# A fused convolution and feed-forward kernel on Trainium2: blocks 2 and 3 convolved in bf16 quarter tiles, and two chunks of F in one PSUM tile

## The chip, the cores and the metric

The kernel runs on one core of one Trainium2 chip. The metric is device microseconds of one execution; lower is better. A core has TensorE (PE: matmuls; its weight loads are shown apart as PEld), VectorE (DVE), ScalarE (ACT), GpSimd (POOL) and SyncE (SP), each with an instruction queue that it works off in order, and 16 DMA engines. DMAs are issued from the queues of SP, ACT and POOL. SBUF holds 128 partitions of working data; PSUM takes the results of matmuls, in banks of 512 fp32 a partition.

## The reference, cut to what matters

```python
w = softmax(weight, axis=-1)                     # 8 heads x 7 taps
x_unf = x_pad[:, arange(S)[:, None] + arange(7)[None, :], :]   # 6 zeros ahead of each sequence
y = einsum('hk,bskhg->bshg', w, x_unf)           # causal convolution, one set of taps a head
h = y.reshape(32768, 192) @ w_in                 # 192 -> 2048
g = h * (1.0 / (1.0 + exp(-beta * h)))           # beta: one number for each of the 2048
out = g @ w_out                                  # 2048 -> 192
```
There are 8 sequences of 4096 tokens with 192 features; all is fp32 outside, the kernel's matmuls of the two large products are bf16.

## The kernel before, in words

The 32768 tokens are two *streams* of 16384, worked side by side: s = 0 on one half of the partitions, s = 1 on the other. The 192 features are split in three groups of 64 (`NK = 3`, `Q = 64`), so that a convolved tile `xc` has 2 x 64 partitions and three groups by tokens in the free dimensions. F = 2048 is 16 chunks of 128 (`NF`).

The kernel goes through *steps*, ranges of tokens of each stream: step 0 and 1 have 128 tokens, step 2 256, steps 3 to 5 256 each, steps 6 and 7 384, then 512 each. In each step three things are computed:

- the convolution. From step 3 on VectorE does it in seven tap operations (`conv_ops`, L276) on `xt`, the transposed x; the work of later steps stands in a list that `vector_work` (L484) deals out by a budget of nanoseconds for each chunk. For the first four blocks of 128 tokens (steps 0 to 2) TensorE does it: x is transposed on TensorE (`transpose_0`), taken into `xr` in fp32r (`take_0`), and multiplied by seven diagonal matrices `diag` of the taps, one pair of matmuls a tap, one for each stream (`conv_0`, L225). `evac_0` takes the result from PSUM, scaled by `rsum`, to `xcp`.
- mm1: `xc` times w_in, into a PSUM tile `ph` of [128, 2, 512] (two of them rotate), and Silu on ScalarE with the scale `beta`, into `g`. Steps 0 to 2 use `mm1_pair` (L318): chunks u and u + 8 together, chunk u on partition half 0 and u + 8 on half 1, both streams in one moving operand. The others use `mm1` (L333): one chunk a PSUM tile, stream 0 on half 0 and stream 1 on half 1; steps of 256 tokens fill half of the tile.
- mm2: `g` times w_out, in the steps up to 5 by `mm2` (L366): a chunk's 128 rows in two halves, two matmuls of 64x192 for two blocks of 128 tokens, summed over 16 chunks and two phases in two PSUM banks `po`; then `store` copies them out (`o_sp`) and SP writes them. Later steps use `mm2_quarters`, which is untouched. `mm2_plan` (L355) deals four chunks of mm2 of the step before to each chunk of mm1; for steps 0 and 1 the table `first_mm2` (L547) says which chunks of mm2 go behind which unit (i, u).

`mm1_pair` reads only that half of F that lies on its partition half: w_in_s[half 0] holds F 0 to 1023, half 1 the rest. For `mm1` both halves need all of F: `copy_w_in` (L115, issued at L252) copies each half to the other on chip by four DMAs from POOL's queue.

Every instruction is kept in program order on its engine (`pin`), so the order around the change is written by hand. POOL's queue holds, in this order: w_in in six transfers (F 0-255 of each half, 256-639, then the two x loads of blocks 2 and 3 into `xb0`, then 640-1023), w_out_f in four, `xb1` (tokens 512 to 767) in two, `xf` in two, the four copies of w_in_s. `first_tile(i, u)` (L499) says what else is done in steps 0 and 1, behind mm1 of chunk pair u: block 1's convolution at (0,1) and (0,2), its eviction and the transposes of blocks 2 and 3 at (0,3), block 2's convolution at (0,5) and (0,6), block 3's at (1,0) and (1,1), the transposes of xb1 at (1,6), casts and DMA transposes for tile 1 at (1,7). The 16 multiplications of w_out by 1/beta (`scale_w_out`) stand between them on VectorE.

Of the kernel before, what the change touches and what calls it, by code (L numbers as in the profile page):

```python
# [19 lines left out]
def kernel(  # L20
# [25 lines left out]
    def pin(ins):  # L46

        return tc.keep_in_program_order(ins)
# [16 lines left out]

    steps = [(0, 128), (128, 128), (256, 256)]
    NP = len(steps)
# [82 lines left out]
    for f0, f1 in ((0, 256), (256, 640), (640, HF)):  # L150
        for s in range(NS):
            load_w_in(s, HF * s + f0, HF * s + f1)
        if f0 == 256:
            for b in range(2, NB):
                load_x0(b, nc.gpsimd)
# [9 lines left out]
    xr = consts.tile([128, NK, PAD + TILE], FP32R, name="xr")  # L165
# [27 lines left out]
    etap = consts.tile([128, K], FP32, name="etap")  # L193
# [11 lines left out]
    place = [(0, 0), (1, 0), (2, 0), (2, 128)]  # L205
    for i in range(NP):
        xc_of[i] = xc_pool.tile([128, NS, NK, steps[i][1]], BF16, name=f"xcp{i}", bufs=1)
# [10 lines left out]
    def take_0(t, b, act=False):  # L218
        dst = xr[:, :, PAD + 128 * b:PAD + 128 * b + 128]
        if act:  # L220
            pin(nc.scalar.activation(dst, t, AF.Copy))
        else:
            pin(nc.vector.tensor_copy(dst, t))
# [9 lines left out]
    def evac_0(cv, b, s, eng, k0=0, k1=NK):  # L233
        i, c = place[b]
        src = cv[s][:, 128 * k0:128 * k1].rearrange("p (k t) -> p k t", t=128)
        dst = xc_of[i][:, s, k0:k1, c:c + 128]
        if eng is nc.scalar:
            pin(nc.scalar.activation(dst, src, AF.Copy, scale=rsum))
        else:
            pin(eng.tensor_scalar_mul(dst, src, rsum))  # L240
# [11 lines left out]
    for f in range(0, HF, 512):  # L252
        for s in range(NS):
            copy_w_in(s, HF * s + f, HF * s + f + 512)
# [15 lines left out]
    pin(nc.vector.tensor_scalar_mul(tapn, etap, rsum))  # L270

# [61 lines left out]
    def mm1(i, fc):  # L333


        n = steps[i][1]
        ph = psum_h.tile([128, NS, TILE], FP32, name="ph")
        parts = [(0, 128)] if i <= NQ else [(0, 64), (64, 128)]
        for kk in range(NK):
            for m0, m1 in parts:  # L340
                for s in range(NS):
                    pin(nc.tensor.matmul(ph[m0:m1, s, 0:n],  # L342
                                         w_in_s[half_of(s), kk, 128 * fc + m0:128 * fc + m1],
                                         xc_of[i][half_of(s), kk, 0:n],
                                         start=(kk == 0), stop=(kk == NK - 1)))
        pin(nc.scalar.activation(g_at(i, fc)[:, :, 0:n], ph[:, :, 0:n], AF.Silu,  # L346
                                 scale=beta[:, fc:fc + 1]))
# [34 lines left out]
    def store(i, pr, po):  # L382
# [5 lines left out]
        if sa == sb:  # L388
# [110 lines left out]
    def first_tile(i, u):  # L499
# [4 lines left out]
        elif (i, u) == (0, 3):  # L504
            t23 = [transpose_0(pa[b], xb0, b) for b in range(2)]
            for b in range(2):
                take_0(t23[b], 2 + b)
            for s in range(NS):
                evac_0(pb, 1, s, nc.vector)
        elif (i, u) == (0, 5):  # L510
            conv_0(pa, 2, 0, 4)
            for c in range(4):
                scale_w_out(c)
        elif (i, u) == (0, 6):
            conv_0(pa, 2, 4, K)
            for s in range(NS):
                evac_0(pa, 2, s, nc.vector)
            for c in range(4, 8):
                scale_w_out(c)
        elif (i, u) == (1, 0):  # L520
            conv_0(pb, 3, 0, 4)
        elif (i, u) == (1, 1):
            conv_0(pb, 3, 4, K)
            for s in range(NS):
                evac_0(pb, 3, s, nc.vector)
            for c in range(8, NF):
                scale_w_out(c)
        elif (i, u) == (1, 6):
            new_xt(1)
            ts_ = [transpose_0(pb[b], xb1, b) for b in range(2)]  # L530
            for b in range(2):
                pin(nc.vector.tensor_copy(xt_of[1][:, :, LEAD + 128 * b:LEAD + 128 * b + 128], ts_[b]))
            pin(nc.vector.tensor_copy(xt_of[0][:, :, TILE + LEAD - PAD:],
                                      xr[:, :, TILE:].bitcast(FP32)))
# [13 lines left out]
    for key, us, cuts in (((0, 0), [(1, u) for u in range(2, 8)], (0, 3, 6, 9, 12, 13, 16)),  # L548
                          ((1, 0), [(2, 1), (2, 2)], (0, 8, 16)),
                          ((0, 1), [(2, 3), (2, 4)], (0, 8, 16)),  # L550
                          ((1, 1), [(2, 5), (2, 6), (2, 7)], (0, 5, 10, 16))):
        for (i, u), c0, c1 in zip(us, cuts, cuts[1:]):
            first_mm2[(i, u) + key] = range(c0, c1)

    for i in range(n_steps):
        plan = mm2_plan(i - 1) if NP <= i <= NQ else [[] for _ in range(NF)]
        new_g(i, 0)
        if i < NP:
            new_g(i, 1)
        if i < NP:  # L560
            for u in range(NF // 2):
                mm1_pair(i, u)
                first_tile(i, u)
                for ph in (0, 1):
                    for j in range(i):
                        for fc in first_mm2.get((i, u, j, ph), ()):
                            mm2(j, prs_0, ph, fc)
                if i == 2:
                    vector_work(i, 1300, flush=u == NF // 2 - 1)
            continue  # L570
        for u in range(NF):
            if u == NF // 2:
                new_g(i, 1)
            mm1(i, u)
            for t in plan[u]:
                mm2(i - 1, *t)
                if t[1] == 1 and t[2] == NF - 1:
                    budget -= 2 * (D + 60) / 0.96
            if i > NQ:
                mm2_quarters(NM)  # L580
            vector_work(i, 1307 * steps[i][1] // TILE, flush=u == NF - 1)
# [30 lines left out]
```

## Time and profile before

| | |
|---|---|
| five runs | 686.74, 687.43, 687.5, 687.4, 686.19 us; median 687.4 |
| the profiled execution | 686.74 us; span 685.0 us, 1.74 us outside the span |
| granted TensorE clock | 1.000 |
| TensorE busy | 679.1 us, 99% of the span |
| ScalarE, VectorE busy | 585.4 us (85%), 551.4 us (81%) |
| POOL busy | 14.6 us |

The page's numbers are of one execution. Busy time of TensorE is time in which any matmul is in flight, with modelled ends, so the gaps between starts say more than the share. "Idle before" of an instruction is the time its engine did nothing just before it, with the releaser that ended it. The timeline view merges neighbours of one line, so a row's length can reach over rows of another line. The view of DMA issues gives the time from issue to landing. The first 32 us hold steps 0 to 2; step 3 begins at 30.68 us, step 4 at 41.7, step 5 at 52.3, step 6 at 62.84 and step 7 at 76.27.

### The profile page before, as it was taken

The numbers are of one execution on the slowest core, as the hardware profiler recorded it, in microseconds if no ns is written. First come the engines' busy times: TensorE is split into PE (matmuls) and PEld (weight loads), VectorE is DVE, ScalarE is ACT, GpSimd is POOL, SyncE is SP. The second block draws the span as 40 slices with busy tenths as digits, with TensorE's granted clock in tenths as the row PEclk, the third lists the DMA queues.
The fourth block names the chain that finished last, engine by engine and source line by source line (L and its number), as shares of the span: only waits on it lengthen the run. The fifth ranks groups of instructions, "written<-read, shape, count | busy, mean of one in ns | idle before, by whom it ended". The sixth has DMA issues, their size and how long they took to land.

```text
span 685.0 us, 27204 instructions
## 1 busy us (share of the span) xinstructions
PE 679.1 (99%) x12528; PEld 460.0 (67%) x12528; DVE 551.4 (81%) x886; ACT 585.4 (85%) x585; POOL 14.6 (2%) x26
## 2 busy tenths in 40 slices
PE   8999999999999999999999999999999999999998
PEld 6799887666666666666666666666666666666667
DVE  5999999999988889878889888889888889875112
ACT  7999999888888888888888888888888888888881
POOL 8000000000000000000000000000000000000000
PEclk9999999999999999999999999999999999999999
DMA  9753444344423344423444323344323443220223
GB/s 203 185 131 92 121 110 118 85 117 117 117 61 82 103 109 117 117 53 85 106 112 117 96 63 97 100 118 117 87 58 105 105 117 72 67 51 4 49 48 94
DMA packets 150418, 66.85 MB, mean 98 GB/s; under 512 B 113648, under 2 KB 149696, under 8 KB 150304
## 3 DMA queue, kind: packets, MB, share of 16 engines
q1 hardware_dynamic: 146992, 61.08, 35.1%
q0 software_dynamic: 3168, 3.93, 2.8%
q8 instruction: 98, 1.61, 1.1%
q14 instruction: 16, 0.13, 0.1%
q10 hardware_dynamic: 144, 0.10, 0.1%
HBM read 28.32 MB, written 25.17 MB: 78 GB/s over the span
## 4 chain that ended last, share of the span: by engine, by line
PE 97%; DMA 1%; POOL 1%; ACT 1%; issue 0%; DVE 0%; POOLq 0%
PE ph L342 47%; PE po L420 43%; PE po L374 4%; PE po L458 2%; PE ph L325 1%; DMA w_in_s<-in_moe_w_in_dram 1%; ACT g L329 1%; POOL w_in_s L113 0%; PE po L229 0%; ACT gp L329 0%; POOL xb L131 0%; PE po L215 0%; POOL sel L146 0%; DVE o_sp L380 0%; POOL ident L148 0%
## 5 line engine op out<-in xcount | busy, mean ns | idle before, releaser
L346 ACT ACTIVATE g<-ph,beta 128x1024 bf16<-128x1024 f32 (+2 forms) x528 | 558.6, 1063 | 80.0 <-PE ph L342 62.0
L342 PE MATMUL ph<-xc,w_in_s 64*64 64x512 bf16 (+3 forms) x5952 | 617.5, 368 | 0.3 <-ACT g L329 0.3
L420 PE MATMUL po<-g,w_out_s 64*64 64x512 bf16 (+1 forms) x5568 | 580.9, 372 | 0.0
L342 PEld LDWEIGHTS <-w_in_s 64*64 64x64 bf16 (+1 forms) x5952 | 274.9, 104 | 126.0 <-issue 0.5
L420 PEld LDWEIGHTS <-w_out_s 64*64 64x64 bf16 x5568 | 290.1, 118 | 83.8
L303 DVE SCALAR_TENSOR_TENSOR acc<-xt,tapn,acc 128x512 f32<-128x512 bf16 (+2 forms) x450 | 311.4, 768 | 0.9
L437 DVE STREAM_TRANSPOSE o_sb<-po 128x512 f32<-128x512 f32 (+1 forms) x87 | 76.5, 880 | 112.1 <-PE po L420 112.0
L303 DVE SCALAR_TENSOR_TENSOR xc<-xt,tapn,acc 128x512 bf16<-128x512 bf16 (+2 forms) x90 | 64.2, 770 | 0.2
L87 DVE CAST xb<-xf 128x768 bf16<-128x768 f32 (+1 forms) x62 | 48.6, 824 | 0.2 <-DMA xf<-in_x_dram 0.2
L301 DVE TENSOR_SCALAR acc<-xt,tapn 128x512 f32<-128x512 bf16 (+2 forms) x90 | 41.1, 486 | 1.1
L374 PE MATMUL po<-w_out_s,g 64*128 64x192 bf16 x512 | 32.6, 243 | 0.0
L374 PEld LDWEIGHTS <-g 64*128 64x128 bf16 x512 | 24.8, 94 | 1.6
L325 PE MATMUL ph<-xcp,w_in_s 64*128 64x256 bf16 (+1 forms) x144 | 14.9, 306 | 0.8 <-DMA w_in_s<-in_moe_w_in_dram 0.6
L380 DVE COPY o_sp<-po 128x192 f32<-128x192 f32 x28 | 9.0, 353 | 8.0 <-PE po L458 7.3
L329 ACT ACTIVATE gp<-ph,beta 128x256 bf16<-128x256 f32 x32 | 12.8, 477 | 2.0 <-PE ph L325 1.8
L458 PEld LDWEIGHTS <-g 128*128 128x128 bf16 x128 | 10.5, 98 | 0.4 <-issue 0.4
L458 PE MATMUL po<-w_out_s,g 128*128 128x192 bf16 x128 | 10.7, 246 | 0.0
L329 ACT ACTIVATE g<-ph,beta 128x512 bf16<-128x512 f32 x16 | 9.6, 693 | 0.1
L325 PEld LDWEIGHTS <-w_in_s 64*128 64x128 bf16 x144 | 6.7, 94 | 4.4 <-issue 1.6
L374 PE MATMUL po<-w_out_s,gp 64*128 64x192 bf16 x128 | 7.5, 243 | 0.0
L374 PEld LDWEIGHTS <-gp 64*128 64x128 bf16 x128 | 5.9, 94 | 1.6
L229 PE MATMUL po<-xr,diag 64*128 64x384 f32 x49 | 7.0, 360 | 0.0
(52 smaller groups left out, 56.6 us busy)
## 6 DMA issues: line engine op xcount, KB each, us to landing
xf<-in_x_dram SPq DMA_DIRECT2D x60, 384.0 KB, 4.2
out_dram<-o_sb SPq DMA_DIRECT2D x108, 192.0 KB, 4.6
xt<-xb SPq DMA_TRANSPOSE x122, 3.1
out_dram<-o_sp SPq DMA_DIRECT2D x10, 192.0 KB, 3.7
w_out_f<-in_moe_w_out_dram POOLq DMA_DIRECT2D x4, 384.0 KB, 6.8
out_dram<-o_sb SPq DMA_DIRECT2D x8, 144.0 KB, 4.7
w_in_s<-w_in_s POOLq DMA_DIRECT2D x4, 192.0 KB, 7.8
out_dram<-o_sp SPq DMA_DIRECT2D x8, 96.0 KB, 1.8
```

The costliest lines, as they stand in the source:

```text
L87: pin((eng or nc.vector).tensor_copy(xbf_of[j][:, b0:b1, :, s, :].rearrange("p b k q -> p k b q"), xf_of[j][:, b0:b1, s, :].rearrange("p b ...
L301: pin(nc.vector.tensor_scalar_mul(a, src, w))
L303: pin(nc.vector.scalar_tensor_tensor(out=xc_of[i][:, k0:k1, o:o + m] if k == K - 1 else a, in0=src, scalar=w, in1=a, op0=ALU.mult, op1=ALU ...
L325: pin(nc.tensor.matmul(ph[:, h, 0:NS * n], w_in_s[half_of(h), kk, ts(fcs[h], 128)], xc_of[i][half_of(h), :, kk, :], start=(kk == 0), stop= ...
L329: pin(nc.scalar.activation(g_at(i, fcs[h])[:, :, 0:n], ph[:, h, 0:NS * n].rearrange("p (s t) -> p s t", s=NS), AF.Silu, scale=beta[:, fcs[ ...
L342: pin(nc.tensor.matmul(ph[m0:m1, s, 0:n], w_in_s[half_of(s), kk, 128 * fc + m0:128 * fc + m1], xc_of[i][half_of(s), kk, 0:n], start=(kk == ...
L346: pin(nc.scalar.activation(g_at(i, fc)[:, :, 0:n], ph[:, :, 0:n], AF.Silu, scale=beta[:, fc:fc + 1]))
L374: pin(nc.tensor.matmul(po[q][:, 0:D], g_at(i, fc)[r, s, ts(b, 128)], w_out_s[r, fc, :], start=(phase == 0 and fc == 0), stop=(phase == 1 a ...
L380: pin(nc.vector.tensor_copy(dst, po[:, 0:D]))
L420: pin(nc.tensor.matmul(po_of[i, m][half_of(s), 0:n], w_out_s[half_of(r), fc, m:D:NM], g_at(i, fc)[half_of(r), s, 0:n], start=(first and fc ...
L437: pin(nc.vector.transpose(osb_of[i][:, 0:n // L, :, m], po_of[i, m][:, 0:n].rearrange("p (b l) -> p b l", l=L)))
L458: pin(nc.tensor.matmul(po[:, 0:D], g_at(i, fc)[:, s, ts(b, 128)], w_out_s[:, fc, :], start=(fc == 0), stop=(fc == NF - 1)))
```

## The change

Blocks 0 and 1 are done as before. Blocks 2 and 3 are taken into a new bf16 tile `xrb`; their taps are split in two bf16 parts each (`tap2`: the tap, and what its rounding leaves), 14 diagonals `diag_b` in bf16, made by one VectorE instruction. `conv_23` multiplies them in quarter tiles (64 rows by 64 columns): block 2 goes to partition half 0 and block 3 to half 1, both streams in separate banks. The result `xcq` has the block as partition half, and both streams in its free dimension, so step 2 now goes through `mm1`, like the later steps, with the copies of w_in_s, and no longer through `mm1_pair`.

`mm1` takes a list of chunks: in steps of 256 tokens two chunks share one PSUM tile, and their mm2 follow behind both. The list of what is done where is written anew: the x loads of blocks 2 and 3 come behind all of w_in in POOL's queue; the copies of w_in_s are issued half by half; the transposes of blocks 2 and 3 move to (0,6) and (0,7), their convolution to (1,0) to (1,4), three diagonals each and two at last; the transposes of xb1 move from (1,6) to (1,5), with eight of the w_out multiplications behind them; mm2 of steps 0 and 1 gets another table.

```diff
     steps = [(0, 128), (128, 128), (256, 256)]
-    NP = len(steps)
+    ND, NP = 2, len(steps)
...
     for f0, f1 in ((0, 256), (256, 640), (640, HF)):
         for s in range(NS):
             load_w_in(s, HF * s + f0, HF * s + f1)
-        if f0 == 256:
-            for b in range(2, NB):
-                load_x0(b, nc.gpsimd)
+    for b in range(2, NB):
+        load_x0(b, nc.gpsimd)
...
-    xr = consts.tile([128, NK, PAD + TILE], FP32R, name="xr")
+    xr = consts.tile([128, NK, PAD + 256], FP32R, name="xr")
...
-    etap = consts.tile([128, K], FP32, name="etap")
+    tap2 = consts.tile([128, 2, K], FP32, name="tap2")
+    etap = tap2[:, 0, :]
...
+    for i in range(ND):
+        xc_of[i] = xc_pool.tile([128, NS, NK, 128], BF16, name=f"xcp{i}", bufs=1)
+    xc_of[ND] = xc_pool.tile([128, NK, NS, 128], BF16, name="xcq", bufs=1)
...
+        xd, c = (xr, PAD + 128 * b) if b < 2 else (xrb, PAD + 128 * (b - 2))
+        dst = xd[:, :, c:c + 128]
...
+    def conv_23(cv, k0, k1):
+        for k in range(k0, k1):
+            for c in range(2):
+                for s in range(NS):
+                    t = 128 * c + k % K
+                    pin(nc.tensor.matmul(
+                        cv[s][half_of(c), 0:NK * 128], diag_b[half_of(s), k, :],
+                        xrb[half_of(s), :, t:t + 128], start=(k == 0), stop=(k == 2 * K - 1)))
...
-    for f in range(0, HF, 512):
-        for s in range(NS):
+    for s in range(NS):
+        for f in range(0, HF, 512):
             copy_w_in(s, HF * s + f, HF * s + f + 512)
...
+    tap_b = consts.tile([128, K], BF16, name="tap_b")
+    pin(nc.vector.tensor_copy(tap_b, etap))
+    pin(nc.vector.tensor_tensor(out=tap2[:, 1, :], in0=etap, in1=tap_b, op=ALU.subtract))
+    diag_b = consts.tile([128, 2 * K, Q], BF16, name="diag_b")
+    pin(nc.vector.tensor_tensor(
+        out=diag_b, in0=ident2[:, None, 0, :].to_broadcast([128, 2 * K, Q]),
+        in1=tap2.rearrange("p a k -> p (a k)")[:, :, None].to_broadcast([128, 2 * K, Q]), op=ALU.mult))
+    xrb = consts.tile([128, NK, PAD + 256], BF16, name="xrb")
+    pin(nc.vector.tensor_copy(xrb[:, :, 0:PAD], xr[:, :, 256:].bitcast(FP32)))
...
-    def mm1(i, fc):
+    def mm1(i, fcs):
         n = steps[i][1]
         ph = psum_h.tile([128, NS, TILE], FP32, name="ph")
         parts = [(0, 128)] if i <= NQ else [(0, 64), (64, 128)]
+        for e, fc in enumerate(fcs):
+            for kk in range(NK):
+                for m0, m1 in parts:
+                    for s in range(NS):
+                        rhs = xc_of[i][half_of(s), kk, :, :] if i == ND else xc_of[i][half_of(s), kk, 0:n]
+                        pin(nc.tensor.matmul(ph[m0:m1, s, n * e:n * e + n],
+                                             w_in_s[half_of(s), kk, 128 * fc + m0:128 * fc + m1], rhs,
+                                             start=(kk == 0), stop=(kk == NK - 1)))
+        for e, fc in enumerate(fcs):
+            pin(nc.scalar.activation(g_at(i, fc)[:, :, 0:n], ph[:, :, n * e:n * e + n], AF.Silu,
+                                     scale=beta[:, fc:fc + 1]))
...
         elif (i, u) == (0, 3):
-            t23 = [transpose_0(pa[b], xb0, b) for b in range(2)]
-            for b in range(2):
-                take_0(t23[b], 2 + b)
             for s in range(NS):
                 evac_0(pb, 1, s, nc.vector)
-        elif (i, u) == (0, 5):
-            conv_0(pa, 2, 0, 4)
-            for c in range(4):
-                scale_w_out(c)
...
+        elif (i, u) in ((0, 6), (0, 7)):
+            b = u - 6
+            take_0(transpose_0(pa[b], xb0, b), 2 + b)
+        elif i == 1 and u < 5:
+            conv_23(pb, 3 * u, min(3 * u + 3, 2 * K))
+            if u == 0:
+                for c in range(8):
+                    scale_w_out(c)
+            elif u == 4:
+                for s in range(NS):
+                    evac_0(pb, 2, s, nc.vector)
+        elif (i, u) == (1, 5):
             new_xt(1)
             ts_ = [transpose_0(pb[b], xb1, b) for b in range(2)]
             for b in range(2):
                 pin(nc.vector.tensor_copy(xt_of[1][:, :, LEAD + 128 * b:LEAD + 128 * b + 128], ts_[b]))
             pin(nc.vector.tensor_copy(xt_of[0][:, :, TILE + LEAD - PAD:],
-                                      xr[:, :, TILE:].bitcast(FP32)))
+                                      xrb[:, :, 256:]))
+            for c in range(8, NF):
+                scale_w_out(c)
...
-    for key, us, cuts in (((0, 0), [(1, u) for u in range(2, 8)], (0, 3, 6, 9, 12, 13, 16)),
-                          ((1, 0), [(2, 1), (2, 2)], (0, 8, 16)),
-                          ((0, 1), [(2, 3), (2, 4)], (0, 8, 16)),
-                          ((1, 1), [(2, 5), (2, 6), (2, 7)], (0, 5, 10, 16))):
+    for key, us, cuts in (((0, 0), [(1, 6), (1, 7), (2, 0)], (0, 5, 10, 16)),
+                          ((1, 0), [(2, u) for u in range(2, 6)], range(0, 17, 4)),
+                          ((0, 1), [(2, u) for u in range(6, 10)], range(0, 17, 4)),
+                          ((1, 1), [(2, u) for u in range(10, 16)], (0, 2, 5, 8, 10, 13, 16))):
...
-        for u in range(NF):
+        du = 2 if steps[i][1] == 256 else 1
+        for u in range(0, NF, du):
+            us = range(u, u + du)
             if u == NF // 2:
                 new_g(i, 1)
-            mm1(i, u)
-            for t in plan[u]:
-                mm2(i - 1, *t)
+            mm1(i, us)
+            for v in us:
+                mm2_first(v)
+                for t in plan[v]:
+                    mm2(i - 1, *t)
...
-            vector_work(i, 1307 * steps[i][1] // TILE, flush=u == NF - 1)
+            vector_work(i, 1307 * du * steps[i][1] // TILE, flush=u + du == NF)
```

## The prediction

> **What bounds the kernel now.** I read the busy shares first, then the chain that ended last, then each engine's order of time in the first 32 us, since the change reaches no further than step 6.
>
> ```profile
> PE 679.1 (99%) x12528; PEld 460.0 (67%) x12528; DVE 551.4 (81%) x886; ACT 585.4 (85%) x585; POOL 14.6 (2%) x26
> ```
> ```profile
> PE 97%; DMA 1%; POOL 1%; ACT 1%; issue 0%; DVE 0%; POOLq 0%
> ```
> TensorE sets the end. From step 3 on it issues one chunk every 0.66 us without a gap, and later stages also show no wait, so a change in the head moves the end by as much as it moves step 3's stream. The head is different. TensorE, in order of time (start, length, what, idle before it and its releaser):
>
> ```profile
> 12.33 0.39 PE L325 MATMUL ph<-xcp,w_in_s 64*128 64x256 bf16 x4 [0.59 <-DMA w_in_s<-in_moe_w_in_dram]
> ...
> 17.33 0.49 PE L325 MATMUL ph<-xcp,w_in_s 64*128 64x256 bf16 x6
> ...
> 20.16 0.49 PE L215 MATMUL po<-ident_b,xb 128*128 128x128 bf16 x6
> 20.59 0.26 PE L374 MATMUL po<-w_out_s,gp 64*128 64x192 bf16 x2
> ...
> 21.25 1.67 PE L325 MATMUL ph<-xcp,w_in_s 64*128 64x512 bf16 x12
> ...
> 30.68 0.50 PE L342 MATMUL ph<-xc,w_in_s 64*128 64x256 bf16 x6
> 31.01 0.51 PE L374 MATMUL po<-w_out_s,g 64*128 64x192 bf16 x8
> 31.84 0.39 PE L342 MATMUL ph<-xc,w_in_s 64*128 64x256 bf16 x4 [0.32 <-ACT g L329]
> ```
> Step 3 starts at 30.68, but its second chunk comes 1.16 us later instead of 0.66: it waits for a PSUM tile, so the stream counts as if begun at 31.18. ScalarE in the same stretch:
>
> ```profile
> 8.08 4.22 ACT L329 ACTIVATE gp<-ph,beta 128x256 bf16<-128x256 f32 x10 [0.85 <-PE ph L325]
> 12.86 0.84 ACT L329 ACTIVATE gp<-ph,beta 128x256 bf16<-128x256 f32 x2 [0.56 <-PE ph L325]
> 13.92 7.13 ACT L329 ACTIVATE gp<-ph,beta 128x256 bf16<-128x256 f32 x18 [0.22 <-PE ph L325]
> 21.21 0.84 ACT L329 ACTIVATE gp<-ph,beta 128x256 bf16<-128x256 f32 x2 [0.16 <-PE ph L325]
> 22.11 9.68 ACT L329 ACTIVATE g<-ph,beta 128x512 bf16<-128x512 f32 x16
> ```
> It is nearly full from 8 to 32 us: the head goes at ScalarE's pace, and its one large hole is at 12.3, where the third part of w_in lands. VectorE, for step 3's tokens:
>
> ```profile
> 20.52 0.62 DVE L532 COPY xt<-po 128x384 bf16<-128x384 bf16 x2 [0.21 <-PE po L215]
> ...
> 22.48 0.75 DVE L301 TENSOR_SCALAR acc<-xt,tapn 128x768 f32<-128x768 bf16 x1
> 23.27 4.18 DVE L303 SCALAR_TENSOR_TENSOR acc<-xt,tapn,acc 128x768 f32<-128x768 bf16 x4
> 27.56 0.62 DVE L380 COPY o_sp<-po 128x192 f32<-128x192 f32 x2
> 28.10 1.01 DVE L303 SCALAR_TENSOR_TENSOR acc<-xt,tapn,acc 128x768 f32<-128x768 bf16 x1
> 29.14 1.02 DVE L303 SCALAR_TENSOR_TENSOR xc<-xt,tapn,acc 128x768 bf16<-128x768 bf16 x1
> ```
> Its last tap ends at 30.16, half a microsecond before step 3's first matmul. Two transfers matter, from the view of issues taken around each (KB, us from issue to landing):
>
> ```profile
> xb<-in_x_dram POOLq DMA_DIRECT2D x1, 96.0 KB, 9.3
> ```
> ```profile
> w_in_s<-w_in_s POOLq DMA_DIRECT2D x1, 192.0 KB, 8.8
> ```
> The first is the second half of xb1 (tokens 512 to 767), issued at 10.71: it lands at 20.0, and the transposes that read it start at 20.16. The second is the first copy of w_in_s to the other half, issued at 13.48: it lands at 22.3. The other copies land at 22.8, 23.4 and 23.9 (issues at 14.68, 15.88, 19.56; 8.1, 7.5, 4.3 us).
>
> **The change, part by part.**
>
> *POOL's queue.* The last w_in part takes the place of the two x loads and is issued 1.45 us earlier (4.33 instead of 5.78), so it should land near 10.8 instead of 12.29. The x loads move past it and land 1 to 2.5 us later (9.2 and 9.9 before, so at most 12.4); their transposes now stand at chunk pairs 6 and 7 of step 0, after 12.5. ScalarE's 0.56 and 0.22 us holes go. Nothing behind in the queue moves: the bytes ahead are the same.
>
> *Convolution of blocks 2 and 3.* Removed: 28 matmuls of 64x384 in steps 0 and 1, 14 pairs 0.18 us apart (the rows of the first block, 5.22, 5.40, 5.58), 2.5 us. Added: 56 quarter matmuls of 64x384 in 14 rounds of four. That form is not in the head; in step 8 twelve quarter matmuls of 384 columns take 0.49 us (95.80 to 96.29), 0.163 a round, so 2.3 us. What the ten changes between half and quarter tiles in (1,0) to (1,4) cost has one near row: where step 7 goes from half to quarter tiles at 76.27, eight mm2 matmuls were followed after 0.44 us instead of 0.33. I take that 0.11, 1.1 us in all. Ends: nothing, and ten times the 0.21 to 0.27 us that weight loads sat idle before the 128-row transposes at 10.46 and 20.13, 2.4 us.
>
> The Trainium skill (TensorEngine Tiling (Array Packing), Key Properties) says that a change of tiling mode drains TensorE, which speaks against putting ten of them into step 1. The trace agrees in kind. The page has no price; if each drain were as long as a half-tile matmul's 0.27 us, an estimate from this trace, the step would take 2.7 us more, against 1.1 by the row at 76.27.
>
> *VectorE.* Added: two small taps operations (0.2 us each by the row at 8.35), the 128x896 product (between 0.3 us, a 128x128 product, and 1.42 us, a 128x1152 tap; I take 1.1), a 0.16 us copy; removed: two evictions, 1.14 us. They lie in the 2.36 us that VectorE stood idle up to 10.92; without that cover block 1's eviction would slip by 1.8 us against its use near 13.9, still in time.
>
> *The early gain, and the gate that takes it.* Without the hole, and with two convolutions fewer between the chunk pairs (paired activations come every 0.72 us where nothing delays them, 0.88 where a convolution does), step 1 starts about 1.3 us sooner. TensorE then runs conv taps from about 14.3 (the eighth pair's transposes, plus 0.55 for VectorE's copy), 0.33 + 0.49 + 0.22 us a pair, ends the taps near 18.8 and mm1 of (1,5) near 19.3. There stand the xb1 transposes, one pair earlier than before, with two gates: xb1 lands at 20.0 as before, and their PSUM banks are free when VectorE has evicted the convolution, 18.9 + 1.14, also near 20.05. Queued behind them on TensorE: mm1 of (1,6) and (1,7) and all of mm2; ScalarE runs dry near 20. The 1.3 us are lost and more: of the work that had been done by then, one mm1 (0.33) and twelve mm2 chunks (0.99) are missing.
>
> From 20.05 on: transposes 0.43, mm1 (1,6) 0.33, five mm2 chunks 0.41 (16 matmuls, eight chunks, take 0.66), mm1 (1,7) 0.33, five chunks 0.41: 21.96. Step 2 now needs both halves of w_in_s, so its second matmul waits for the first copy, 22.3; the others are in time. Step 2 itself: eight pairs of mm1 at 0.65 (16 chunks of 512 columns) and 54 mm2 chunks at 0.0825: 5.2 + 4.46 = 9.66. Step 3 starts at 31.96. ScalarE needs 0.57 to 0.60 us an activation, 9.4 for 16, less than TensorE's 9.66, so no wait is left in front of step 3. Against 31.18: **+0.78**.
>
> VectorE meanwhile: transposes' copies 20.4 to 20.95, tail 0.16, then eight w_out chunks that used to come before them (0.25 each, 2.0), casts 0.83, halo 0.2, taps 0 to 4 0.79 + 4.18, the o_sp pair 0.54 (its mm2 ends near 28.7), two taps 2.06: 31.7. That is 0.25 us before TensorE; a slower piece here comes through in full.
>
> *Two chunks a tile, steps 3 to 5.* 24 pairs: 1.314 us before; step 2's pairs, the same columns, are 1.305 to 1.31 apart: 0 to −0.2, I take **−0.1**. From below, were the whole 0.017 us by which a chunk exceeds its columns (1,536 columns take step 8 0.64 us) to go, 48 chunks give −0.8.
>
> *Order on VectorE.* In step 5 the o_sp pair comes one tap earlier, and three taps of 0.645 instead of two now follow its wait. The last tap ended at 62.23, step 6 began at 62.84: **+0.1**.
>
> Sum: +0.8. The profiled execution took 686.74, so 687.5; the median of 687.4 is 0.66 above that execution, so the forecast is **688.2**. 0.2% (1.4 us) is about what a measurement of this kernel can tell from no change.
>
> **Rivals.**
> *Slower: the taps and their eviction become the gate, or the copies land late.* With 0.24 us a mode change, a pair takes 1.30 instead of 1.04, the taps end at 19.9, the eviction at 21.1, and all behind it comes 1.1 later. Or the first copy slips: w_out_f's four transfers, alike in size, landed after 6.2 to 10.0 us, so 1 to 2 us is in range, and each beyond 22.3 moves step 2 in full. Either gives +1.8 to +2.8: 689.2 to 690.2. It decides from 0.6 us on. For it: two gates fall together at 20.05, so nothing is spare. Against: the queue's bytes are unchanged, and the nearest row has 0.11.
> *Faster: xb1 and the copies land earlier.* With waits like the shortest rows (4.3 and 4.9 us) neither transfer gates. TensorE's own work then allows step 2 from 19.6 (ScalarE's 16 pairs at 0.72 from 8.08) and step 3 at 29.3, VectorE allows 30.6: −0.6 to −1.9, with pairing −0.7 to −2.0: 685.4 to 686.7. For it: POOL's last copy took 4.3 us. Against: all landings from 18 to 24 us come in queue order.
> *No effect: the early gain and the late work cancel.* If the first copy lands by 21.9, its 0.34 us goes; if the banks come free at 19.8 and xb1 lands at 19.7, another 0.3: +0.1 to +0.5, 687.5 to 687.9.
>
> **How the numbers follow.** Forecast case 0.43, of it 0.30 under +1.4 and 0.13 over; slower rival 0.30; faster rival 0.20, of it 0.13 beyond −1.4; no effect 0.07. So faster 0.13, same 0.30 + 0.07 + 0.07 = 0.44, slower 0.43. The range, 686.3 to 690.2, goes from inside the faster rival to the slower rival's end and leaves some 0.13 below and 0.06 above.
>
> **What would show it.** Right: no hole on ScalarE near 12.3; a hole of 0.5 to 1.5 us on ScalarE between 19 and 21.5, the xb1 transposes at 20.0 to 20.3; the first matmul on xcq not before 22.2; step 3 near 32.0 with no wait for ScalarE. Wrong: transposes before 19.5 or after 20.8, quarter matmuls over 0.18 us a round, or a VectorE wait at step 3 or step 6 over 0.3 us.

## The result and the profile after

| | before | after |
|---|---|---|
| median | 686.75 us (45 runs, 685.86 to 687.59) | 687.93 us (25 runs, 687.04 to 688.97) |
| ratio | | 1.0017, 95% interval 1.0011 to 1.0022 |
| profiled execution, span | 686.74, 685.0 us | 687.91, 686.1 us |
| step 2, step 3, step 6, step 7 start | 21.25, 30.68 (counts as 31.18), 62.84, 76.27 | 22.31, 32.24, 63.99, 77.42 |

The change costs 1.18 us, 0.17%. The forecast time of 688.2 us lies 0.27 above what was measured. From the page of the changed kernel, the busy time and the chain that ended last by engine: TensorE is still the bound, and nothing else has more than 1% of the chain.

```profile
PE 680.2 (99%) x12604; PEld 461.5 (67%) x12604; DVE 550.8 (80%) x888; ACT 584.2 (85%) x585; POOL 14.5 (2%) x26
```
```profile
PE 98%; DMA 1%; POOL 0%; ACT 0%; DVE 0%; issue 0%; POOLq 0%
```

From step 6 to step 7 both kernels take 13.43 us, and both spans end 608.7 us after step 7 starts. All of the difference is made before 64 us. TensorE in the head, in order of time (start, length, what, idle before it and its releaser):

```profile
9.60 0.39 PE L346 MATMUL ph<-xcp,w_in_s 64*128 64x256 bf16 x4 [0.55 <-DMA w_in_s<-in_moe_w_in_dram]
...
15.21 0.50 PE L346 MATMUL ph<-xcp,w_in_s 64*128 64x256 bf16 x6
15.64 0.69 PE L242 MATMUL po<-xrb,diag_b 64*64 64x384 bf16 x12
16.27 0.50 PE L346 MATMUL ph<-xcp,w_in_s 64*128 64x256 bf16 x6
...
19.25 0.50 PE L346 MATMUL ph<-xcp,w_in_s 64*128 64x256 bf16 x6
20.03 0.33 PE L216 MATMUL po<-ident_b,xb 128*128 128x128 bf16 x3 [0.28 <-DVE xcq L252]
20.56 0.33 PE L216 MATMUL po<-ident_b,xb 128*128 128x128 bf16 x3 [0.20 <-DVE xcq L252]
20.82 0.50 PE L346 MATMUL ph<-xcp,w_in_s 64*128 64x256 bf16 x6
21.16 0.58 PE L397 MATMUL po<-w_out_s,gp 64*128 64x192 bf16 x10
21.57 0.49 PE L346 MATMUL ph<-xcp,w_in_s 64*128 64x256 bf16 x6
21.90 0.58 PE L397 MATMUL po<-w_out_s,gp 64*128 64x192 bf16 x10
22.31 1.01 PE L365 MATMUL ph<-xcq,w_in_s 64*128 64x256 bf16 x12
...
32.24 0.83 PE L365 MATMUL ph<-xc,w_in_s 64*128 64x256 bf16 x12
32.89 0.84 PE L397 MATMUL po<-w_out_s,g 64*128 64x192 bf16 x16
```

Read it from the bottom. Step 3 starts at 32.24 with no wait behind it, 1.06 later than the 31.18 that counted before. Step 2 starts at 22.31. Ahead of it stand four rows without a gap, and ahead of these the xb1 transposes (L216), in two parts of three, each released by VectorE's eviction of the convolution. The hole that w_in made at 12.3 has gone, but there is a new one at 9.6. ScalarE and VectorE in the same stretch:

```profile
10.14 5.37 ACT L350 ACTIVATE gp<-ph,beta 128x256 bf16<-128x256 f32 x14 [0.73 <-PE ph L346]
...
21.36 1.58 ACT L350 ACTIVATE gp<-ph,beta 128x256 bf16<-128x256 f32 x4 [0.73 <-PE ph L346]
```
```profile
8.43 1.09 DVE L287 TENSOR_TENSOR diag_b<-ident,tap 128x896 bf16<-128x896 f32 x1
...
19.36 1.14 DVE L252 TENSOR_SCALAR xcq<-po,rsum 128x384 bf16<-128x384 f32 x2 [2.98 <-PE po L242]
...
30.70 1.02 DVE L324 SCALAR_TENSOR_TENSOR xc<-xt,tapn,acc 128x768 bf16<-128x768 bf16 x1
...
63.22 0.62 DVE L324 SCALAR_TENSOR_TENSOR xc<-xt,tapn,acc 128x384 bf16<-128x384 bf16 x1
```

ScalarE runs dry at 20.6 for 0.73 us, behind the transposes. VectorE finishes step 3's tokens at 31.72, half a microsecond ahead of TensorE; for step 6 its last tap ends at 63.84 and TensorE starts at 63.99. The transfers, from the view of DMA issues around each (KB, us from issue to landing): the later transfer of w_in's second part, issued at 3.70, with the first of its third part; the two of xb1, issued at 10.58 and 11.34; the first copy of w_in_s, issued at 13.61.

```profile
w_in_s<-in_moe_w_in_dram POOLq DMA_DIRECT2D x2, 144.0 KB, 5.9
```
```profile
xb<-in_x_dram POOLq DMA_DIRECT2D x2, 96.0 KB, 8.7
```
```profile
w_in_s<-w_in_s POOLq DMA_DIRECT2D x1, 192.0 KB, 8.8
```

Taken alone, the later transfer of xb1 took 8.6 us and landed at 19.94; the first of the two evictions (the row at 19.36 holds both) ended at 19.98. The two events that the first transposes need lie 0.04 us apart in this execution, and the second transposes wait for the second eviction, which ended at 20.51.

### The profile page after: what moved, and what is told of

Read it like the earlier page. It is cut to its first block, busy times and chain, and to the rows that moved or that the text cites. A ratio compares the mean times of both kernels' runs of the same rounds, so it can differ in the third digit from the quotient of the medians.

```text
span 686.1 us, 27363 instructions
## 1 busy us (share of the span) xinstructions
PE 680.2 (99%) x12604; PEld 461.5 (67%) x12604; DVE 550.8 (80%) x888; ACT 584.2 (85%) x585; POOL 14.5 (2%) x26
## 4 chain that ended last, share of the span: by engine, by line
PE 98%; DMA 1%; POOL 0%; ACT 0%; DVE 0%; issue 0%; POOLq 0%
PE ph L365 48%; PE po L445 43%; PE po L397 4%; PE po L483 2%; DMA w_in_s<-in_moe_w_in_dram 1%; PE ph L346 1%; PE po L242 0%; POOL w_in_s L114 0%; ACT gp L350 0%; DVE xcq L252 0%; PE po L216 0%; PE po L231 0%; POOL sel L147 0%; DVE o_sp L403 0%; POOL ident L149 0%
## 5 line engine op out<-in xcount | busy, mean ns | idle before, releaser
L369 ACT ACTIVATE g<-ph,beta 128x1024 bf16<-128x1024 f32 (+2 forms) x544 | 566.9, 1052 | 81.5 <-PE ph L365 62.2
L365 PEld LDWEIGHTS <-w_in_s 64*64 64x64 bf16 (+1 forms) x6048 | 280.5, 104 | 125.6 <-issue 0.4
L397 PE MATMUL po<-w_out_s,g 64*128 64x192 bf16 x512 | 28.3, 243 | 0.0
L346 PE MATMUL ph<-xcp,w_in_s 64*128 64x256 bf16 x96 | 8.4, 272 | 1.2 <-ACT gp L350 0.6
L365 PE MATMUL ph<-xcq,w_in_s 64*128 64x256 bf16 x96 | 7.4, 269 | 0.0
L346 PEld LDWEIGHTS <-w_in_s 64*128 64x128 bf16 x96 | 4.0, 94 | 4.4 <-issue 2.7
L312 DVE COPY xt<-xt 128x18 bf16<-128x18 bf16 x28 | 4.5, 159 | 0.0
```

The lines of the kernel that those rows point to most:

```text
L346: pin(nc.tensor.matmul(ph[:, h, 0:NS * n], w_in_s[half_of(h), kk, ts(fcs[h], 128)], xc_of[i][half_of(h), :, kk, :], start=(kk == 0), stop= ...
L365: pin(nc.tensor.matmul(ph[m0:m1, s, n * e:n * e + n], w_in_s[half_of(s), kk, 128 * fc + m0:128 * fc + m1], rhs, start=(kk == 0), stop=(kk ...
L369: pin(nc.scalar.activation(g_at(i, fc)[:, :, 0:n], ph[:, :, n * e:n * e + n], AF.Silu, scale=beta[:, fc:fc + 1]))
L397: pin(nc.tensor.matmul(po[q][:, 0:D], g_at(i, fc)[r, s, ts(b, 128)], w_out_s[r, fc, :], start=(phase == 0 and fc == 0), stop=(phase == 1 a ...
```

## The experiments

The theory on trial: the loss lies before step 3, in (a) two gates in front of the xb1 transposes that fall together (the landing of xb1, and the taps with their eviction), and (b) the chunks of mm2 that now come after those gates; sharing PSUM tiles is a gain of about half a microsecond, which pays part of it. The rivals: sharing the tiles is itself what costs; the transfers alone gate; the new order of w_in costs; the places of mm2 cost nothing.

Single executions are compared with care, because the start of the first mm1 moved by up to 1.6 us between executions (last section). Medians are given with the ratio to the kernel before on the same chip. In the first four runs the kernel before had 686.55 us, in the next four 686.83, in the last 686.73.

### Shared PSUM tiles alone

```diff
-        for u in range(NF):
+        du = 2 if steps[i][1] == 256 else 1
+        for u in range(0, NF, du):
...
+            us = range(u, u + du)
...
-            mm1(i, u)
+            mm1(i, us)
```
(on the kernel before, with mm1's new form; the work of VectorE is dealt out once for two chunks, as in the changed kernel)

> The kernel before with one part of the change alone: steps 3 to 5 put two chunks into one PSUM tile. Theory (the pairing is worth only the wait before step 3): step 3's first pair finds a free PSUM tile, so the 0.5 us wait for ScalarE at 31.84 goes; two chunks stay at 1.31 us; step 6 begins 0.1 to 0.2 us late behind VectorE. Step 6's first matmul at 62.5 instead of 62.84, time 0.3 to 0.5 us under the kernel before. Rival (the pairing itself costs the 1.1 us): step 6's first matmul at 63.5 or later, time 0.7 to 1.2 us above the kernel before.

Measured: 686.39 us, ratio 0.9997 (0.9987 to 1.0006). TensorE, in order of time:

```profile
31.31 0.83 PE L344 MATMUL ph<-xc,w_in_s 64*128 64x256 bf16 x12
31.97 0.84 PE L376 MATMUL po<-w_out_s,g 64*128 64x192 bf16 x16
32.63 0.83 PE L344 MATMUL ph<-xc,w_in_s 64*128 64x256 bf16 x12
```

The second row of mm1 follows after 1.32 us for two chunks, so the 0.5 us wait for ScalarE that stood in step 3 is gone. This execution's first mm1 began at 8.72, 1.2 us later than that of the kernel before, so its absolute times say little; from step 3 to step 6 it took 31.75 us, against 31.66 before (62.84 less 31.18), because step 6 waited about 0.2 us for VectorE's last tap. The median is 0.16 lower, less than the 0.3 to 0.5 expected and within what can be told. That sharing costs the 0.7 to 1.2 us of the rival is excluded; the interval ends at 0.0006, 0.4 us.

### The changed kernel without sharing in steps 3 to 5

```diff
-        du = 2 if steps[i][1] == 256 else 1
+        du = 2 if i == ND else 1
```

> The changed kernel with one chunk a PSUM tile in steps 3 to 5 again. Theory: step 3 begins at 32.2 as in the changed kernel, its second chunk waits 0.5 us for ScalarE, and step 6's late tap of 0.15 us goes: 0.3 us above the changed kernel. Rival (the pairing itself is slow): 0.8 to 1.1 us below the changed kernel.

Measured: 688.83 us (five runs), ratio 1.0033 (1.002 to 1.0045).

```profile
33.32 0.50 PE L365 MATMUL ph<-xc,w_in_s 64*128 64x256 bf16 x6 [0.32 <-ACT g L369]
```

Step 3 began at 32.17; its second chunk came 1.15 us later instead of 0.66, with ScalarE as releaser: the stall is back, and step 6 starts at 64.32 instead of 63.99. From 32.66 (33.32 less 0.66) to step 6 it takes 31.66, as in the kernel before, and there is no wait at step 6. Sharing is worth 0.5 for the stall and 0.1 in the 48 chunks; the wait that it brings at step 6 takes 0.2 back. Sharing helps the changed kernel too. How much is less sure: the medians differ by 0.90, where 0.3 was expected and the profiled executions differ by 0.30 (688.21, the fastest of the five runs, and 687.91); where the rest of the 0.90 comes from is open.

### The transfers earlier

```diff
-    for c in range(0, NF, 4):
-        pin(nc.gpsimd.dma_start(out=w_out_f[:, c:c + 4, :], in_=w_out_v[:, c:c + 4, :]))
+    for c in (0, 4):
+        load_w_out(c)
...
+    copy_w_in(0, 0, 512)
+    for c in (8, 12):
+        load_w_out(c)
```
(xb1's two transfers stand between the two loops)

> The changed kernel with xb1 and the first copy of w_in_s ahead of the last two w_out_f transfers in POOL's queue. Theory (two gates fall together, xb1's landing and the eviction of the taps): xb1 lands near 17 and the copy near 18, but the transposes of xb1 still start at 20.0 behind the eviction, the second at 20.5; step 2's wait of 0.1 us goes; step 3 at 32.1, time 0 to 0.2 us below the changed kernel. Rival (the landing of xb1 is the gate): transposes before 19.6, step 3 at 31.6 or earlier, time 0.5 us or more below the changed kernel.

Measured: 687.9 us, ratio 1.0022 (1.0012 to 1.0031): no better than the changed kernel. The two xb1 transfers, issued at 8.55 and 10.10, took 6.8 us at the median and the later one 6.1, so both had landed by 16.3; the copy, issued at 10.84, took 6.0 and landed by 17. TensorE and VectorE, in order of time:

```profile
20.85 0.33 PE L222 MATMUL po<-ident_b,xb 128*128 128x128 bf16 x3 [0.28 <-DMA w_in_s<-w_in_s]
21.38 0.33 PE L222 MATMUL po<-ident_b,xb 128*128 128x128 bf16 x3 [0.20 <-DVE xcq L258]
```
```profile
20.18 1.14 DVE L258 TENSOR_SCALAR xcq<-po,rsum 128x384 bf16<-128x384 f32 x2 [2.59 <-PE po L248]
```

The transposes still come 0.67 us after the eviction starts, as in the changed kernel (19.36 and 20.03). The releaser named in the first row is a transfer of w_in_s, which a transpose of xb1 does not read: a wait is put down to the event that came last, and here the one that fits is the first half of the eviction, over at 20.80. So the second gate alone holds them here. But this execution began its first mm1 at 8.72, which put the eviction 0.82 later than in the changed kernel's profile and past that kernel's landing of xb1 (19.94), so it would look the same without the edit. It is also one of the two slowest of the nine runs (688.87): VectorE waited 0.9 us for a load of x near 34 us, and step 6 then waited 0.37 us for its last tap. That the rival of the transfers alone falls rests on the median, 687.9, where it had 0.5 us or more under the changed kernel's 687.93.

### The taps in two groups of seven

```diff
-        elif i == 1 and u < 5:
-            conv_23(pb, 3 * u, min(3 * u + 3, 2 * K))
+        elif i == 1 and u in (0, 2):
+            conv_23(pb, K * u // 2, K * u // 2 + K)
```

> The changed kernel with the 14 rounds of taps in two groups of seven, behind (1,0) and (1,2), so that TensorE goes to quarter tiles and back twice instead of five times and the eviction ends near 19.1. Theory (two gates): the first transposes of xb1 start at 20.0 behind the landing; the second no longer waits (0.2 us), then the first copy of w_in_s holds step 2 at 22.3 to 22.4; step 3 at 32.1 to 32.2, time 0 to 0.2 us below the changed kernel. Rival (the quarter tiles and their eviction are the gate alone): transposes near 19.6, step 3 at 31.6 or earlier.

Measured: 687.86 us, ratio 1.0019 (1.001 to 1.0028): the same as the changed kernel. The eviction moves from 19.36 to 18.31, and the six transposes come together at 20.07, without an eviction wait. In the profiled execution neither gate was the one that held them: xb1 had landed by 18.6, the first mm1 began late, at 8.28, and ScalarE's pace released (1,5) at 19.63. So this profile does not show the landing as the gate that is left; that rests on the medians of this run and of the next. With xb1 there early and the taps out of the way, this execution took 687.38 and began step 3 at 31.75, 0.49 ahead of the changed kernel's profile although its first mm1 came 1.12 later. That fits two gates that must both be out of the way.

### Both at once

```diff
+    copy_w_in(0, 0, 512)
...
+        elif i == 1 and u in (0, 2):
+            conv_23(pb, K * u // 2, K * u // 2 + K)
```
(the two edits above together)

> The changed kernel with both gates moved at once: the second x load and the first copy of w_in_s ahead of the last two w_out_f transfers, and the 14 rounds of taps in two groups of seven. Theory (two gates tie near 20.05, so that moving one alone gives nothing): the xb1 transposes start between 19.0 and 19.6 in an execution whose first mm1 starts near 7.2, step 2 follows 0.6 to 1.0 us earlier than the changed kernel's 22.31; then VectorE, held by the later w_out_f transfers, allows step 3 from about 31.4 instead of 32.24, and the time falls by 0.4 to 0.8, to 687.1 to 687.5. Rival (the two gates are not the cause, ScalarE's pace or something later is): within 0.2 of the changed kernel, 687.7 to 688.1.

Measured: 687.35 us, ratio 1.0005 (0.9997 to 1.0014): 0.5 to 0.6 under each of the two alone and under the changed kernel. (Against the kernel before on the same chip it is +0.52, each of the two alone +1.35 and +1.31.) Its first mm1 began at 7.17 and that of the changed kernel at 7.16, so the rows can be compared as they stand:

```profile
19.35 0.50 PE L351 MATMUL ph<-xcp,w_in_s 64*128 64x256 bf16 x6 [0.60 <-ACT gp L355]
19.79 0.52 PE L222 MATMUL po<-ident_b,xb 128*128 128x128 bf16 x6
...
21.73 0.82 PE L370 MATMUL ph<-xcq,w_in_s 64*128 64x256 bf16 x12
...
31.47 0.83 PE L370 MATMUL ph<-xc,w_in_s 64*128 64x256 bf16 x12
```

Against the changed kernel step 2 starts 0.58 earlier (22.31 there; just under the 0.6 to 1.0 expected), step 3 0.77 earlier, the span is 0.8 shorter (685.3). In the medians one gate moved gives nothing and both give 0.6 us: that is how two tied gates behave. The other 0.19 to step 3 lies inside step 2, and goes with the copy that was moved along: step 2 takes 9.74 us here and in the profiles of the three other variants of the changed kernel above, all without a wait for the copy, against 9.93 in the changed kernel, where the copy landed after step 2 had begun. The interval of this ratio and that of the changed kernel (1.0011 to 1.0022) overlap a little, so the rows of the two profiles weigh more than the medians here. The transposes missed the expected 19.0 to 19.6 by 0.2: ScalarE is next. It had holes of 0.92 and 0.47 us behind the two groups of taps, and TensorE waits for it at 19.35.

### VectorE's order of before, with shared tiles

```diff
-            vector_work(i, 1307 * du * steps[i][1] // TILE, flush=u + du == NF)
+                vector_work(i, 1307 * steps[i][1] // TILE, flush=v == NF - 1)
```
(the kernel before with shared tiles; the work of VectorE is dealt out once per chunk v, behind that chunk's mm2)

> The kernel before with two chunks a PSUM tile in steps 3 to 5, and VectorE's work dealt out once per chunk, so that VectorE's order is that of the kernel before. Theory (the 0.2 us wait at the start of step 6 comes from VectorE's new order alone): no wait at step 6, 0.2 less than with pairs alone (686.39), so 686.1 to 686.3, and 0.3 to 0.5 under the kernel before. Rival (the wait comes from step 3's earlier stream, whatever the order): the wait stays, 686.3 to 686.5.

Measured: 686.7 us, ratio 0.9991 (0.9982 to 1.0). VectorE and TensorE, in order of time:

```profile
61.62 0.62 DVE L303 SCALAR_TENSOR_TENSOR xc<-xt,tapn,acc 128x384 bf16<-128x384 bf16 x1
```
```profile
62.85 0.67 PE L344 MATMUL ph<-xc,w_in_s 64*128 64x384 bf16 x6
```

The tap ends 0.61 us ahead of step 6, and from step 3 (31.29) to step 6 it takes 31.56: no wait, 0.19 less than with shared tiles alone. The wait at step 6 comes from VectorE's order, as the theory has it. In the medians it does not show (686.39 with the wait, 686.7 without, above both expected ranges): 0.2 us is under what eleven runs can tell.

### The changed kernel without its quarter tiles

```diff
-        if f0 == 256:
-            for b in range(2, NB):
-                load_x0(b, nc.gpsimd)
+    for b in range(2, NB):
+        load_x0(b, nc.gpsimd)
...
-        elif (i, u) == (0, 5):
+        elif (i, u) == (0, 7):
             conv_0(pa, 2, 0, 4)
...
-        elif (i, u) == (1, 0):
+        elif (i, u) == (1, 1):
             conv_0(pb, 3, 0, 4)
```
(the kernel before with shared tiles, VectorE's work dealt out per chunk and POOL's new order; the transposes of blocks 2 and 3 move to (0,5), block 2's taps to (0,7) and (1,0), block 3's to (1,1) and (1,2); half tiles in fp32r, mm2 and xb1 in their old places)

> The kernel before with POOL's new order (all of w_in ahead of the x loads), pairs dealt out per chunk, and blocks 2 and 3 convolved in half tiles as before, each one to two pairs later: the changed kernel without its quarter tiles. Theory (the reordering of w_in is worth nothing while xb1 lands at 20.0; the loss in the changed kernel comes from what stands between that landing and step 2, and from the copies that step 2 must then wait for): transposes at 20.0 to 20.2, step 2 at 21.1 to 21.3, step 3 at 30.6 to 30.8 without a stall behind it, 686.0 to 686.3. Rival (w_in's new order is itself what costs, through its second part landing 0.8 us later): 687.0 to 687.9.

Measured: 686.4 us, ratio 0.9996 (0.9988 to 1.0005). Its interval and that of the changed kernel (1.0011 to 1.0022) do not meet.

```profile
20.11 0.52 PE L214 MATMUL po<-ident_b,xb 128*128 128x128 bf16 x6
...
21.23 1.67 PE L324 MATMUL ph<-xcp,w_in_s 64*128 64x512 bf16 x12
...
30.65 0.83 PE L343 MATMUL ph<-xc,w_in_s 64*128 64x256 bf16 x12
```

The starts are those expected, the time 0.1 above the range. w_in's new order is not what costs. Nor does it bring anything measurable: the hole at 12.3 is gone, a smaller one for the second part of w_in stands at 9.37 (0.22 on TensorE, 0.42 on ScalarE). The transposes follow (1,5) with no wait at all, and xb1 had landed by 18.9, so here the pace of the pairs, and no landing, sets their place.

### The same, with xb1 earlier

```diff
+    for c in (0, 4, 8):
+        load_w_out(c)
...
+    load_w_out(12)
...
-    for key, us, cuts in (((0, 0), [(1, u) for u in range(2, 8)], (0, 3, 6, 9, 12, 13, 16)),
+    for key, us, cuts in (((0, 0), [(1, 2), (1, 3), (1, 4), (1, 5), (1, 7), (2, 0)], (0, 3, 6, 9, 12, 14, 16)),
```
(xb1's two transfers stand ahead of the last load; the last four w_out chunks are scaled behind the xb1 copies)

> As half_tiles, with xb1 loaded ahead of the last w_out_f transfer, the last four w_out chunks scaled after the xb1 copies, and the last chunks of the first mm2 moved to the start of step 2. Theory (xb1's landing gates step 2 in half_tiles): transposes by 19.5, step 2 at 20.3 to 20.7; VectorE, which waits for the xf loads (landing 21.4 to 21.9) and needs 8.7 us from there to step 3's tokens, allows step 3 at 30.2 to 30.5: 685.5 to 685.9, under both kernels. Rival (ScalarE or VectorE sets step 3 whatever xb1 does): as half_tiles, 686.0 to 686.3.

Measured: 687.09 us, ratio 1.0 (0.9991 to 1.0009). Both expectations were wrong. TensorE and VectorE, in order of time:

```profile
21.83 0.49 PE L379 MATMUL po<-w_out_s,gp 64*128 64x192 bf16 x4 [0.41 <-DVE w_out_s L276]
```
```profile
21.47 1.00 DVE L276 TENSOR_SCALAR w_out_s<-w_out_f,rbeta 128x192 bf16<-128x192 f32 x4
```

The transposes came at 20.46, again with no wait for a transfer (the first mm1 had begun at 8.09), so there was no gate to remove. The edit made one of its own instead: mm2 of chunk 12 stands in front of step 2 and waits for a multiplication that now comes behind the xb1 copies.

### Half tiles, with the changed kernel's places for mm2

```diff
-    for key, us, cuts in (((0, 0), [(1, u) for u in range(2, 8)], (0, 3, 6, 9, 12, 13, 16)),
+    for key, us, cuts in (((0, 0), [(1, 6), (1, 7), (2, 0)], (0, 5, 10, 16)),
```

> As half_tiles (686.4), but with the changed kernel's places for the first 16 chunks of mm2: five in (1,6), five in (1,7), six at the start of step 2, instead of three a pair from (1,2) on. No gate and no quarter tile is added. Theory (what the changed kernel loses is in part cover: mm2 chunks that ran while ScalarE set the pace of step 1 now run where TensorE sets it): twelve chunks move behind the xb1 transposes, up to 0.99 us, of which ScalarE's pace in (1,6) and (1,7) still hides some; step 3 at 31.2 to 31.6 instead of 30.65, 686.9 to 687.4. Rival (the places of mm2 cost nothing, only the gates in front of the transposes do): 686.2 to 686.6.

Measured: 687.09 us, ratio 1.0005 (0.9996 to 1.0014), 0.69 above half tiles with mm2 in its old places.

```profile
20.06 0.52 PE L214 MATMUL po<-ident_b,xb 128*128 128x128 bf16 x6
20.51 0.59 PE L375 MATMUL po<-w_out_s,gp 64*128 64x192 bf16 x10
20.93 0.49 PE L324 MATMUL ph<-xcp,w_in_s 64*128 64x256 bf16 x6
...
21.67 0.81 PE L324 MATMUL ph<-xcp,w_in_s 64*128 64x512 bf16 x6
...
31.37 0.83 PE L343 MATMUL ph<-xc,w_in_s 64*128 64x256 bf16 x12
```

The transposes start where they did (20.06 against 20.11), since ScalarE paces what is ahead of them. Everything behind them is TensorE's own work, and there is more of it: step 3 comes at 31.37 instead of 30.65, 0.72 later, inside the expected 31.2 to 31.6. The rival that the places of mm2 cost nothing falls.

### The account

Four profiled executions whose first mm1 began within 0.1 us of each other (7.16 to 7.26), and the medians beside them:

| kernel | step 2 | step 3 | step 6 | span | median |
|---|---|---|---|---|---|
| half tiles, shared, mm2 early | 21.23 | 30.65 | 62.21 | 684.3 | 686.4 |
| the same, mm2 late | 21.67 | 31.37 | 62.92 | 685.1 | 687.09 |
| quarter tiles, both gates moved | 21.73 | 31.47 | 63.22 | 685.3 | 687.35 |
| the changed kernel | 22.31 | 32.24 | 63.99 | 686.1 | 687.93 |

Against step 6 of the kernel before (62.84): -0.63 for shared tiles (0.53 in front of step 3, 0.10 in steps 3 to 5), +0.72 for mm2's late places (step 3), +0.10 more to step 3 with the quarter tiles and step 2 through `mm1`, +0.77 for the two gates (step 3; 0.58 of it in front of step 2, 0.19 inside it, with the copy), +0.19 for the wait at step 6: +1.15, which is what the profile of the changed kernel has. The kernel before began its first mm1 at 7.53, some 0.3 later than these four; what that is worth in the first term is not known.

The first row of the table is the change without its quarter tiles and without what came with them (mm2's and xb1's places, step 2 through `mm1`); its 0.4 us under the kernel before cannot be told from nothing (0.9988 to 1.0005). No version tried is clearly faster than the kernel before; nearest are shared tiles with VectorE's order of before (0.9982 to 1.0) and this one.

## Why the prediction was right or wrong

**The sum: mechanism right, size 0.4 too small, on a base 0.65 too high.** The forecast was +0.8 on the median of five runs, 687.4. Forty-five runs of the kernel before put its median at 686.75, and the change added 1.18. The two errors nearly cancel, so that the forecast time came within 0.27 is luck; 687.93 lies in the range for the reason forecast, but the cost itself was forecast a third too small. The terms that were too small are step 2's length, 9.93 instead of 9.66, and the wait at step 6, 0.19 instead of 0.1: together 0.36 of the 0.38, by the rows of the profiled execution. The signs named for a right forecast all came: no hole on ScalarE near 12.3, one of 0.73 at 20.6, the transposes at 20.03, the first matmul on xcq at 22.31, and no wait behind step 3's start.

**POOL's queue: half right.** The hole at 12.3 went. The forecast said that w_in's third part would land early and looked no further: that part's neighbour, the second part, landed at about 9.6 (3.70 plus 5.9 us) where it had taken 5.0 us before (4.9 to 5.1 in the three profiled executions with the old order, 5.1 to 6.1 in the eight with the new), and made holes of 0.55 on TensorE and 0.73 on ScalarE at 9.6 and 10.1. So (1,0) began at 14.10, 0.71 ahead of the kernel before (14.81), not 1.3, and 0.37 of this was an earlier first mm1. The run with half tiles has the same order and a smaller hole, and no measurable gain.

**Convolution of blocks 2 and 3: right.** A pair with taps took 1.05 us (15.21 to 16.27; forecast 1.04). In its rows mm1's 0.33 is followed by 0.10 until the taps start, and three rounds of 0.163 by 0.14 until mm1 starts: 0.12 a change of mode, against the 0.11 taken from the row at 76.27. The Trainium skill's rule (TensorEngine Tiling (Array Packing), Key Properties) that a change of tiling mode drains TensorE agrees in kind. The page has no price; the prediction's estimate of 0.27 us each would have put a pair at 1.36, which the rows refute.

**VectorE's added work: right.** The 128x896 product took 1.09 us (forecast 1.1) in idle time; step 3's tokens were ready at 31.72 (forecast 31.7).

**The early gain and the gate that takes it: right in kind, the gate 0.45 late.** Both gates were named, and the runs show the pair: either one moved gives nothing, both give 0.6. But the eviction was forecast from 18.9 to 20.05 and ran from 19.36 to 20.5, so the second bank came free near 20.5. Half of the 0.45 is the new hole at 9.6: the taps began at 14.53 instead of 14.3. The transposes, forecast as one block of 0.43 from 20.05, went in two halves from 20.03 and took 0.79 until mm1 of (1,6). That step failed in size, by 0.36, but it did not lengthen the sum: the forecast had TensorE ready for step 2 at 21.96 and waiting for the copy until 22.3, and the 0.36 went into that wait. Where the rival of late taps said 0.6 us or more, 0.45 came: the same mechanism, short of its point.

**From the transposes to step 3: the start of step 2 right in part by luck, its length 0.27 short.** mm1, five chunks, mm1, five chunks took 1.49 us (20.82 to 22.31; forecast 1.48). Step 2 began at 22.31 as forecast, but because TensorE came to it only then, not because it had waited for the copy. The first copy landed at 22.4 (13.61 plus 8.8; forecast 22.3) and cost about 0.1 behind step 2's start, as its first mm1 took 0.74 instead of 0.65. Step 2 lasted 9.93 instead of 9.66: that 0.09, some 0.14 in front of its last mm1, and the rest in pairs of 1.315. ScalarE is the likely cause of the 0.14, though no row names it: the activation that gives the PSUM tile free ended at 31.03, and this mm1 started at 31.08. The forecast had ScalarE in time. In the profiles where the copy was in time, 0.05 is left of the 0.14. Missing mm2 chunks were forecast at twelve and 0.99 us; the run that moves only them costs 0.72.

**Two chunks a tile: right.** -0.1 was taken for the 48 chunks, and 31.56 against 31.66 is what the runs with and without sharing show. That the 0.5 stall goes was in the 31.18.

**Order on VectorE: right, size 0.19 instead of 0.1.** The last tap ended at 63.84, and dealing the work out per chunk takes the wait away.

**The rivals.** The slower one came within 0.15 us of the 0.6 us from which it was to decide. The faster one fell: with xb1 landed by 16.3 and the copy by 17 the changed kernel does not gain, and with the taps' gate moved as well it gets to 687.35, not 685.4 to 686.7. It had TensorE's own work allow step 2 from 19.6; 21.73 was reached, held by ScalarE's pace at 19.35 and by mm2's late places. No effect (+0.1 to +0.5) fell too.

## What to carry to other kernels

Work that runs while another engine sets the pace is free only where it stands: moved behind the next gate, where TensorE is the bound, twelve chunks of mm2 cost 0.72 of their 0.99 us here, and no row shows this as a wait. Where two releasers come at nearly the same time, moving one gave nothing here, and an experiment on one alone would have acquitted both; try them together. A DMA that is brought forward in a queue can take from its neighbours ahead as well as from those it passes (here 0.9 us from w_in's second part): look at the landing of each, not only of the one that moved.

## What the runs showed of the hardware that was not expected

**TensorE starts at little more than half its later pace, and how long it does so differs from execution to execution.** The taps of block 0 are two matmuls of 384 columns side by side. TensorE, in order of time, one row of the kernel before and one of the kernel with shared tiles alone:

```profile
5.40 0.34 PE L229 MATMUL ph<-xr,diag 64*128 64x384 f32 x1
```
```profile
6.57 0.52 PE L229 MATMUL ph<-xr,diag 64*128 64x384 f32 x1
```

In the first execution these rows are 0.18 us apart from 5.22 on, in the second 0.32 us apart up to 7.22; the granted clock is given as 1.00 in both stretches. Over eleven profiled executions the first mm1 began at 7.16, 7.17, 7.24, 7.26, 7.33, 7.53, 8.09, 8.28, 8.72, 8.72 and 8.72 us, and it goes with the kernel's edits in no way that can be seen: the three at 8.72 are two kernels close to the one before and one close to the changed one. The five from 8.09 on have the wide spacing up to 6.9 us or later; the other six have 0.18 us from 5.5 at the latest, and the kernel before is last of these by a wait of 0.37 us for a load of x. The Trainium skill (TensorE: Matmul & The Clock Gate, Part 1) describes a gate that doubles the clock after a window of about 3.4 us in which TensorE was busy, and says that the window runs freely, so that the moment varies with the run. The spacing, 0.32 against 0.18 us, nearly agrees, and a free window would also fit the spread of 1.6 us seen here; no run here tested it. A late start is not passed on in full: the kernel with VectorE's work dealt out per chunk began at 8.72 and reached step 3 at 31.29, 1.48 later at the start than the half-tile kernel and 0.64 later at step 3. Runs of one kernel spread over 1.7 to 1.9 us, and this is a likely part of it; since only one execution of each is profiled, that is argued and not shown.
